# Sliding-window attention into a GEGLU block, groups 2 to 5, second half of the output products: two products change places, the sums' additions and one mask move down the vector engine's queue

## The chip, the cores and the metric

The kernel runs on one core of one Trainium2 chip. The time is the device time of one launch in microseconds (us). A core has five engines with a queue each: PE (matrix multiplications into the 8 banks of PSUM), DVE (vector), ACT (scalar, with the function tables), POOL and SP, which here mostly issue DMAs. Every queue is worked off in the order in which it was written; an instruction whose semaphore is not there yet holds up all behind it on its engine.

## The reference, cut to what matters

```
scores = q @ k.T / sqrt(64)                     # 8 batches, 8 heads, 576 positions, head size 64
scores = scores - slope[h] * (i - j)   where 0 <= i - j < 128, else -1e9
attn   = softmax(scores)                        # rows divided by their sums
x      = (attn @ v), heads side by side         # 4608 tokens x 512
out    = (gelu(x @ w_gate) * (x @ w_val)) @ w_out     # 512 -> 1536 -> 512
```

## The kernel before, in words

The attention works in batches `b` of 576 tokens, the feed-forward block in groups `g` of 512 tokens (nine groups). `xT` holds the attention's result transposed, as a ring of 1536 tokens. Since 576 is not 512, a group's last tokens belong to the next batch: group g+1 needs the first `urgent = 512*(g+2) - 576*(g+1)` tokens of batch g+1, that is 320, 256, 192 and 128 for g = 2, 3, 4, 5. The order of the work on every engine is the order of the Python code (`manual_schedule`); nothing is reordered.

One group has two parts. First come 12 feature tiles (`gate_val`, line 631): four matmuls with `wg` into one bank, four with `wv` into another, then gelu on ACT (L655) and the product `hT` on DVE (L656); tiles 6 to 9 are done together by `gate_quad` with seven products in place of eight (L831 to L878; its sums of `xT` are made on POOL, L789, after tile 3's `hT`). Then comes the product with `w_out`, for groups 2 to 8 also with seven products (`product`, L741 to L752, six matmuls of 128x256 each), for each half `a` of the group's rows. They collect in three banks: products 1, 6, 7, 4 in x, 5 and 3 in y, 2 in z. `gather_out` (L891) takes results out between them, and a bank goes on collecting afterwards:

- p1, u2: copies of x (L898, L900). c11: DVE adds z to what p1 left (L902).
- p5: ACT copies y (L906). c22: DVE adds x, after product 7, to it (L908).
- c21: ACT copies x after product 4 (L910). c12: DVE adds y after product 3 (L913); it is the last reader of y, as c21 is of x.

Into the second half (a = 1, lines 1240 to 1270) are woven: the scores of batch b = g+2 for head pairs 2 and 3 (`scores2`; its list A of ten steps holds the exponentials on ACT, L236, and the masks on DVE, L241: A[2], A[4], A[8], A[9] are masks, the others exponentials); the additions `add(b, 0, None, (0,))` (two instructions on DVE, L391, for the softmax sums of batch b; what they write, `T`, is read by the sums' matmuls, L435, in the next group); and `values(b - 1, urgent=urgent)`, 88 small matmuls (L497) for attn @ v of batch g+1 into six banks, four with one head pair c each and two small ones. Ten scalings on DVE (L556) take these out and divide by the sums: first the urgent part of c = 0, 1, 2, 3 (`scale`), then for the same four banks the rest, which belongs to group g+2, and the two small banks (`more`). So the fifth scaling is the last reader of the bank of c = 0.

The DVE order in this stretch is: u2, c11, two additions, A[2], c22, A[4], ten scalings, c12, A[8], A[9], two more additions, and then `hT` of the next group's tile 0. PE's order is: products 2, 6, 5, 7, the 88 matmuls of `values`, products 3 and 4, and then tile 0 of group g+1. Its first matmul reads `xT` of c = 0, all 512 tokens of the group; the urgent scalings write the last of these.

Banks come from a pool of eight (`bank`, L72). The pool's planner lays the program out with a schedule of its own and gives a new tile the bank that this schedule has had free the longest; a matmul that begins a new tile then waits for the last reader of the tile that had the bank. In the program as laid out, the banks come free after `values`, in each of groups 2 to 5, in the order c = 0, c = 1, x, c = 2, c = 3, the two small ones, y. So tile 0 of group g+1 gets the bank of c = 0 for its `wg` matmuls and the bank of c = 1 for its `wv` matmuls, and tile 1 gets the bank of x and that of c = 2. In the planner's order, counted in PE's matmuls, the fifth scaling begins behind the third matmul of product 4 in group 2, behind the first in group 3, just behind the last matmul of product 3 in group 4 and just ahead of that one in group 5; c21 begins one matmul behind the last of product 4 in all four.

Of the kernel before, what the change touches and what calls it, by code (L numbers as in the profile page):

```python
# [36 lines left out]
def kernel(  # L37
# [346 lines left out]
    def add(b, c0, copy=None, what=(0, 2, 1)):  # L384
        hs = slice(2 * c0, 2 * c0 + 4)
        P = Ps[b % 2].rearrange("p h (n y) -> p h n y", y=64)[:, hs]
        to = T.rearrange("p h (n y) -> p h n y", y=64)[:, hs]
        if 0 in what:
            for x in (0, 1):
                half = slice(64 * x, 64 * x + 64)  # L390
                nc.vector.tensor_tensor(  # L391
                    out=to[half, :, x:x + 7:2], in0=P[half, :, 0:10:3], in1=P[half, :, 1:11:3],
                    op=ALU.add)
        if 2 in what:
            nc.vector.tensor_copy(out=to[0:64, :, 8], in_=P[0:64, :, 12])
            nc.vector.tensor_tensor(
                out=to[64:128, :, 8], in0=P[64:128, :, 11], in1=P[64:128, :, 12], op=ALU.add)
        if 1 in what:
            for x in (0, 1):
                half, n = slice(64 * x, 64 * x + 64), 4 - x  # L400
                (copy or nc.vector.tensor_copy)(
                    out=to[half, :, x + 1:x + 2 * n:2], in_=P[half, :, 2:3 * n:3])
# [270 lines left out]
    def store():  # L673
        for args in stores:
            nc.sync.dma_start(**args)
        stores.clear()
# [64 lines left out]
    def product(g, n, a):  # L741
        (l, r), into = FACTORS[n], INTO[n]
        first = n in (1, 2, 5)
        if first:
            made[g, a, into] = bank()[:, 0:256]
        cols = slice(128 * a, 128 * a + 128)
        x = wo.rearrange("p (i e) (h t) -> p i e h t", e=2, h=2)
        for i in range(NF // 2):
            lhsT = left[:, l, i, cols] if isinstance(l, int) else halves(g)[:, i, l[0], l[1], cols]
            rhs = right[:, r, i, :] if isinstance(r, int) else x[:, i, r[0], r[1], :]  # L750
            nc.tensor.matmul(out=made[g, a, into], lhsT=lhsT, rhs=rhs, start=first and i == 0,  # L751
                             stop=i == NF // 2 - 1, skip_group_check=True)  # L752
# [30 lines left out]
    def combine_x(g, lo=0, hi=256, which=range(4), engine=nc.vector):  # L783
        b11, b12, b21, b22, t1, t2, t3, t4 = (t[:, :, lo:hi] for t in tokens(g) + sums_x(g))
        steps = ((t1, b12, b11, ALU.subtract), (t2, b22, t1, ALU.subtract),
                 (t3, b22, b12, ALU.subtract), (t4, b21, t2, ALU.subtract))
        for n in which:
            to, a, b, op = steps[n]
            engine.tensor_tensor(out=to, in0=a, in1=b, op=op)  # L789
# [101 lines left out]
    def gather_out(g, a, what, copy=nc.scalar.copy):  # L891
        x, y, z = (made.get((g, a, n)) for n in "xyz")
        if what == "p1":
            made[g, a, "lo"] = o_pool.tile([128, DM], FP32, name="osb")
            made[g, a, "hi"] = o_pool.tile([128, DM], FP32, name="osb")
        lo, hi = made[g, a, "lo"], made[g, a, "hi"]
        if what == "p1":
            copy(out=lo[:, 0:256], in_=x)  # L898
        elif what == "u2":
            copy(out=lo[:, 256:512], in_=x)  # L900
        elif what == "c11":
            nc.vector.tensor_tensor(out=lo[:, 0:256], in0=z, in1=lo[:, 0:256], op=ALU.add)  # L902
            if g == NG - 1:
                finished(g, a, lo, slice(0, 256))
        elif what == "p5":
            copy(out=hi[:, 256:512], in_=y)  # L906
        elif what == "c22":
            nc.vector.tensor_tensor(out=hi[:, 256:512], in0=x, in1=hi[:, 256:512], op=ALU.add)  # L908
        elif what == "c21":
            copy(out=hi[:, 0:256], in_=x)  # L910
            finished(g, 2 + a, hi)
        elif what == "c12":
            nc.vector.tensor_tensor(out=lo[:, 256:512], in0=y, in1=lo[:, 256:512], op=ALU.add)  # L913
            finished(g, a, lo, slice(256 if g == NG - 1 else 0, 512), nc.scalar if g == NG - 1 and a else None)
# [229 lines left out]
    def exp_table():  # L1144
        nc.scalar.preload_act_table_set("natural_log_exp_and_others")
# [4 lines left out]
    def out_products(g):  # L1150
        b = g + 2
        O = lambda what, a, copy=act: gather_out(g, a, what, copy)
        P = lambda n, a: product(g, n, a)
        if b > B:
            last = [(4, ("c21",)), (3, ("c12",))]
            for n, after in [(1, ("p1",)), (2, ()), (6, ("u2", "c11")), (5, ("p5",)), (7, ("c22",))] + (
                    last if g == NG - 1 else last[::-1]):
                for a in (0, 1):
                    P(n, a)
                    for what in after:  # L1160
                        O(what, a)
                store()
                if n == 6 and g + 1 < NG:
                    combine_x(g + 1)
            return
        P(1, 0)
        P(2, 0)
        O("p1", 0)
        urgent = 512 * (g + 2) - S * (b - 1)
        if b == B:  # L1170
            P(6, 0)
            O("u2", 0)
            O("c11", 0)
            for n in (3, 2):
                combine_left(g, 0, 6, (n,))
            nc.gpsimd.tensor_copy(out=mark, in_=left[0:1, 2, 5, 0:2])
            sums = combine_weights(0)
            for do in sums[:4]:
                do()
            P(5, 0)  # L1180
            O("p5", 0)
            P(7, 0)
            O("c22", 0)
            scale = values(b - 1, later=True)
            P(4, 0)
            O("c21", 0)
            P(3, 0)
            scale[0]()
            scale[1]()
            O("c12", 0)  # L1190
            P(1, 1)
            O("p1", 1)
            store()
            P(2, 1)
            for do in scale[2:]:
                do()
            combine_x(g + 1, 192, 256, engine=nc.gpsimd)
            for do in sums[4:]:
                do()
            O("c11", 1)  # L1200
            P(6, 1)
            O("u2", 1)
            P(5, 1)
            O("p5", 1)
            P(7, 1)
            O("c22", 1)
            P(3, 1)
            O("c12", 1)
            P(4, 1)
            O("c21", 1)  # L1210
            return
        exp_table()
        O("c11", 0)
        lo = 0 if g == 2 else 2
        combine_left(g, lo, 6, (3,))
        later = []
        scores2(b, 0, later)
        A = later[0]
        P(6, 0)
        O("u2", 0, dve)  # L1220
        combine_left(g, lo, 6, (2,))
        P(5, 0)
        for n in (0, 1, 3):
            A[n]()
        O("p5", 0)
        A[2]()
        P(7, 0)
        O("c22", 0)
        A[4]()
        for n in (5, 6, 7):  # L1230
            A[n]()
        P(1, 1)
        P(4, 0)
        P(3, 0)
        O("p1", 1)
        O("c21", 0)
        O("c12", 0)
        A[8]()
        A[9]()
        scores2(b, 2, later)  # L1240
        A = later[1]
        P(2, 1)
        P(6, 1)
        O("u2", 1, dve)
        O("c11", 1)
        add(b, 0, None, (0,))
        P(5, 1)
        for n in (0, 1, 3, 5, 6, 7):
            A[n]()
        O("p5", 1)  # L1250
        A[2]()
        P(7, 1)
        O("c22", 1)
        A[4]()
        store()
        scale, more = values(b - 1, urgent=urgent)
        for do in scale:
            do()
        P(3, 1)
        P(4, 1)  # L1260
        nc.scalar.preload_act_table_set("gelu_and_others")
        O("c21", 1)
        for do in more:
            do()
        O("c12", 1)
        A[8]()
        A[9]()
        add(b, 0, None, (2,))
        put_off.update({0: lambda: add(b, 0, act, (1,)), 1: lambda: add(b, 2, None, (0, 2)),
                        2: lambda: add(b, 2, act, (1,))})  # L1270
# [3 lines left out]
    for g in range(NG):  # L1274
# [86 lines left out]
        if g in PRODUCTS:  # L1361
            out_products(g)
        else:
            for item in steps(g):
                if isinstance(item, int):
                    out_part(g, item)
                else:
                    RUN[item[0]](*item[1:])
            store()
# [34 lines left out]
```

## Time and profile before

| | us |
|---|---|
| median of 3 runs | 328.53 (328.14 to 328.61) |
| the profiled execution's own time | 328.12 |
| its span from first to last instruction | 326.3 |
| PE busy / DVE busy / ACT busy / POOL busy | 317.3 / 251.7 / 218.2 / 197.1 |
| PE's waits at tile 0 of groups 3 to 6 | 0.77, 0.92, 0.71, 0.51 |

A row of the timeline has the start (us from the span's start), the time from the first start to the last end of a run of equal instructions, the engine, the line of the kernel, the operation, output <- input, shapes (partitions x elements) and the count; in brackets stand the idle time of the engine before it and whose semaphore ended it. The rows of one engine may overlap a little: an instruction is shown until its result is written, and the next one starts before that. A row of the waits has the waiting engine and line, whom it waited for, then the total, the number and the longest.

### The profile page before, as it was taken

To read this page: it belongs to the slowest core of one execution; us is meant where nothing else is said; L and a number is where in the kernel's file an instruction comes from. 1 tells how busy PE (TensorE), PEld (TensorE's weight loads), DVE (VectorE), ACT (ScalarE), POOL (GpSimd) and SP (SyncE) were. 2 spreads that over 40 slices of the span, in tenths; PEclk is the share of its full clock that TensorE was granted. 3 is DMA by queue.
4 is the path that set the end of the run, shared out by engine and by line. 5 is a ranking of instruction groups with operands and counts; after the bars stand their busy time and mean duration, and the time that the engine had idled before them with its cause. 6 is when DMAs were issued, how large, how long until landed. Compare 5 with 4: busy or idle time off the path is not lost. (4 is left out here: it accounts for less than half of the span.)

```text
span 326.3 us, 9416 instructions
## 1 busy us (share of the span) xinstructions
PE 317.3 (97%) x3753; PEld 213.6 (65%) x3753; DVE 251.7 (77%) x499; ACT 218.2 (67%) x417; POOL 197.1 (60%) x228
## 2 busy tenths in 40 slices
PE   8899999999999999999989999999999999999995
PEld 4566746575554768466845785578647787788764
DVE  7889676878779887958797679777896856895692
ACT  7884688567798676756955696578667247627641
POOL 5965589294079896289926994496019495410550
PEclk9999999999999999999999999999999999999999
DMA  8999999999999989966996799769205230003003
GB/s 216 166 195 192 201 174 177 139 192 173 122 152 174 151 150 201 143 133 178 182 186 156 168 128 177 133 167 135 100 35 110 40 131 0 2 0 131 0 4 129
DMA packets 149920, 43.57 MB, mean 134 GB/s; under 512 B 133588, under 2 KB 142964, under 8 KB 149876
## 3 DMA queue, kind: packets, MB, share of 16 engines
q0 software_dynamic: 107456, 18.10, 73.7%
q1 hardware_dynamic: 41424, 23.35, 33.7%
q10 hardware_dynamic: 996, 1.53, 2.0%
q8 instruction: 29, 0.48, 0.6%
q14 instruction: 15, 0.12, 0.2%
HBM read 43.65 MB, written 9.53 MB: 163 GB/s over the span
## 5 line engine op out<-in xcount | busy, mean ns | idle before, releaser
L648 PE MATMUL ps<-xT,wg 128*128 128x512 bf16 (+4 forms) x312 | 71.8, 352 | 2.9 <-DVE xT L556 2.9
L648 PE MATMUL ps<-xT,wv 128*128 128x512 bf16 (+4 forms) x312 | 71.7, 352 | 0.0
L655 ACT ACTIVATE gelu<-ps 128x512 bf16<-128x512 f32 (+3 forms) x77 | 41.6, 546 | 41.7 <-PE ps L648 38.7
L656 DVE TENSOR_TENSOR hT<-ps,gelu 128x512 bf16<-128x512 f32 (+3 forms) x77 | 47.0, 625 | 21.3 <-PE ps L648 15.7
L236 ACT ACTIVATE P<-ps 128x512 bf16<-128x512 f32 (+1 forms) x108 | 51.9, 578 | 4.8 <-PE ps L307 2.5
L648 PEld LDWEIGHTS <-wv 128*128 128x128 bf16 x312 | 29.4, 98 | 29.9 <-DMA wv<-in_moe_w_val_dram 0.3
L648 PEld LDWEIGHTS <-wg 128*128 128x128 bf16 x312 | 28.4, 98 | 30.1 <-DVE xT L556 4.0
L241 DVE TENSOR_TENSOR P<-P,emask 128x768 bf16<-128x768 bf16 x60 | 32.0, 553 | 7.1 <-ACT P L236 5.3
L751 PEld LDWEIGHTS <-hT 128*128 128x128 bf16 x336 | 32.3, 98 | 7.2 <-issue 0.6
L117 POOL DMA_DIRECT2D vb<-in_v_dram x40 | 34.0, 890 | 3.7 <-DMA wo<-in_moe_w_out_dram 1.0
L876 POOL TENSOR_TENSOR hT<-qT,qs 128x512 bf16<-128x512 f32 x10 | 11.5, 1170 | 27.9 <-ACT qs L842 27.9
L117 POOL DMA_DIRECT2D ks<-in_k_dram x30 | 25.4, 885 | 2.8 <-DMA qs<-in_q_dram 2.8
L831 PEld LDWEIGHTS <-kept 128*128 128x128 bf16 x256 | 25.1, 98 | 2.9
L1328 POOL COPY mark<-hT 1x2 bf16<-1x2 bf16 x5 | 0.9, 176 | 42.4 <-DVE hT L656 42.4
L117 POOL DMA_DIRECT2D qs<-in_q_dram x30 | 25.4, 863 | 1.7 <-DMA wo<-in_moe_w_out_dram 1.0
L751 PEld LDWEIGHTS <-left 128*128 128x128 bf16 x252 | 23.8, 98 | 3.7 <-issue 0.4
L751 PE MATMUL ps<-right,hT 128*128 128x256 bf16 x168 | 22.2, 272 | 0.5 <-DVE osb L908 0.2
L839 DVE TENSOR_TENSOR qT<-ps,qT 128x512 f32<-128x512 f32 x20 | 12.9, 686 | 12.5 <-PE ps L831 12.5
L751 PE MATMUL ps<-wo,hT 128*128 128x256 bf16 x168 | 21.0, 273 | 0.0
L751 PE MATMUL ps<-right,left 128*128 128x256 bf16 x168 | 20.6, 273 | 0.2 <-issue 0.2
L839 DVE TENSOR_TENSOR P<-ps,P 128x512 f32<-128x512 f32 x24 | 15.0, 682 | 7.1 <-PE ps L831 7.1
L831 PE MATMUL ps<-xT,wg 128*128 128x256 bf16 x160 | 19.1, 273 | 0.0
(173 smaller groups left out, 616.5 us busy)
## 6 DMA issues: line engine op xcount, KB each, us to landing
out_dram<-osb SPq DMA_DIRECT2D x34, 256.0 KB
rb<-rd SPq DMA_DIRECT2D x8, 576.0 KB
vb<-in_v_dram POOLq DMA_DIRECT2D x32, 128.0 KB, 6.6
qs<-in_q_dram POOLq DMA_DIRECT2D x24, 128.0 KB, 5.5
ks<-in_k_dram POOLq DMA_DIRECT2D x24, 128.0 KB, 7.5
wo<-in_moe_w_out_dram POOLq DMA_DIRECT2D x4, 384.0 KB, 12.1
wg<-in_moe_w_gate_dram POOLq DMA_DIRECT2D x5, 256.0 KB, 9.5
wv<-in_moe_w_val_dram POOLq DMA_DIRECT2D x5, 256.0 KB, 10.1
```

The costliest lines, as they stand in the source:

```text
L117: nc.gpsimd.dma_start(out=t[at:at + n, j, :].rearrange("p (h d) -> p h d", h=H), in_=src[b][:, 128 * j:128 * j + n, :].rearrange("h p d -> ...
L236: nc.scalar.activation(out=dst, in_=src, func=AF.Exp, scale=0.125)
L241: nc.vector.tensor_tensor(out=dst, in0=dst, in1=m, op=ALU.mult)
L648: nc.tensor.matmul(out=ps[:, a:e], lhsT=w[:, c, 128 * f:128 * (f + 1)], rhs=xT[:, c, t0 + lo + a:t0 + lo + e], start=begins and a == 0, st ...
L655: nc.scalar.activation(out=gl[:, 0:n], in_=pg, func=AF.Gelu)
L656: nc.vector.tensor_tensor(out=hid[g][:, f, lo:hi], in0=pv, in1=gl[:, 0:n], op=ALU.mult)
L751: nc.tensor.matmul(out=made[g, a, into], lhsT=lhsT, rhs=rhs, start=first and i == 0, stop=i == NF // 2 - 1, skip_group_check=True)
L831: nc.tensor.matmul(out=ps[:, 256 * e:256 * e + 256], lhsT=w[:, c, at:at + 128], rhs=x[:, c, :], start=n in (1, 2, 5) and e == 0 and c == 0 ...
L839: nc.vector.tensor_tensor(out=to[u], in0=cut(banks[n, u], to[u].shape[1]), in1=to[u], op=ALU.add)
L876: nc.gpsimd.tensor_tensor(out=out, in0=P5[u], in1=high, op=ALU.mult)
L1328: nc.gpsimd.tensor_copy(out=mark, in_=hid[g][0:1, f, 510:512])
```

## The change

Three things are moved in the second half of the output products, in groups 2 to 5. The two additions go from behind c11 to behind c22. The mask A[4] goes from behind c22 to behind the ten scalings, ahead of c12. Product 4 is put ahead of product 3. The instructions themselves stay the same. In the code c21 stays behind both products and ahead of `more` (another engine's queue), and c12 behind A[4].

```diff
         O("u2", 1, dve)
         O("c11", 1)
-        add(b, 0, None, (0,))
         P(5, 1)
         for n in (0, 1, 3, 5, 6, 7):
             A[n]()
         O("p5", 1)
         A[2]()
         P(7, 1)
         O("c22", 1)
-        A[4]()
+        add(b, 0, None, (0,))
         store()
         scale, more = values(b - 1, urgent=urgent)
         for do in scale:
             do()
+        P(4, 1)
         P(3, 1)
-        P(4, 1)
         nc.scalar.preload_act_table_set("gelu_and_others")
         O("c21", 1)
         for do in more:
             do()
+        A[4]()
         O("c12", 1)
         A[8]()
         A[9]()
```

## The prediction

> **What bounds the kernel now.** I read the page's busy shares first, then PE's waits, then the timeline around the end of group 3, then the same places of groups 2, 4 and 5.
>
> ```profile
> PE 317.3 (97%) x3753; PEld 213.6 (65%) x3753; DVE 251.7 (77%) x499; ACT 218.2 (67%) x417; POOL 197.1 (60%) x228
> ```
>
> ```profile
> PE ps L648 <- DVE xT L556: 2.9, 4, 0.9
> ```
>
> PE is the bound: it is busy for 97% of the span. What can be won at all lies in its idle time, and a third of that is one wait that comes four times, 2.9 us together: the first matmul of tile 0 of a group waits for a scaling. The timeline at the end of group 3 shows the place:
>
> ```profile
> 157.64 0.82 PE L751 MATMUL ps<-wo,left 128*128 128x256 bf16 x6
> ...
> 158.50 0.42 DVE L913 TENSOR_TENSOR osb<-ps,osb 128x256 f32<-128x256 f32 x1 [1.09 <-PE ps L751]
> ...
> 161.19 0.82 PE L751 MATMUL ps<-right,hT 128*128 128x256 bf16 x6
> 161.39 1.38 DVE L391 TENSOR_TENSOR T<-P 64x1024 bf16<-64x1024 bf16 x2
> ...
> 162.79 0.56 DVE L241 TENSOR_TENSOR P<-P,emask 128x768 bf16<-128x768 bf16 x1
> 163.27 0.41 DVE L908 TENSOR_TENSOR osb<-ps,osb 128x256 f32<-128x256 f32 x1
> ...
> 163.47 0.83 PE L751 MATMUL ps<-wo,left 128*128 128x256 bf16 x6
> 163.61 0.55 DVE L241 TENSOR_TENSOR P<-P,emask 128x768 bf16<-128x768 bf16 x1
> ...
> 164.07 3.13 DVE L556 TENSOR_TENSOR xT<-ps,rb 128x256 bf16<-128x256 f32 x10
> 164.14 0.82 PE L751 MATMUL ps<-right,hT 128*128 128x256 bf16 x6
> 164.99 0.37 ACT L910 COPY osb<-ps 128x256 f32<-128x256 f32 x1 [1.46 <-PE ps L751]
> ...
> 165.87 1.04 PE L648 MATMUL ps<-xT,wg 128*128 128x512 bf16 x4 [0.92 <-DVE xT L556]
> ...
> 166.74 1.03 PE L648 MATMUL ps<-xT,wv 128*128 128x512 bf16 x4
> ...
> 167.12 0.41 DVE L913 TENSOR_TENSOR osb<-ps,osb 128x256 f32<-128x256 f32 x1
> ```
>
> To be seen: PE ends product 4 at 164.14 + 0.82 = 164.96 and stands until 165.87, while DVE runs from the additions to c12 without a gap (the two additions, A[2], c22, A[4], ten scalings). So in this stretch DVE is what PE waits for. Which of the ten scalings it is, the single rows of the fifth one tell, in groups 2, 3, 4 (with the fourth ahead of it) and 5:
>
> ```profile
> 130.98 0.34 DVE L556 TENSOR_TENSOR xT<-ps,rb 128x192 bf16<-128x192 f32 x1
> ```
> ```profile
> 165.40 0.41 DVE L556 TENSOR_TENSOR xT<-ps,rb 128x256 bf16<-128x256 f32 x1
> ```
> ```profile
> 199.36 0.34 DVE L556 TENSOR_TENSOR xT<-ps,rb 128x192 bf16<-128x192 f32 x1
> ```
> ```profile
> 199.62 0.48 DVE L556 TENSOR_TENSOR xT<-ps,rb 128x320 bf16<-128x320 f32 x1
> ```
> ```profile
> 233.64 0.55 DVE L556 TENSOR_TENSOR xT<-ps,rb 128x384 bf16<-128x384 f32 x1
> ```
>
> and PE's and DVE's rows at the same places of groups 2, 4 and 5:
>
> ```profile
> 126.84 0.82 PE L751 MATMUL ps<-right,hT 128*128 128x256 bf16 x6
> ...
> 129.39 3.13 DVE L556 TENSOR_TENSOR xT<-ps,rb 128x320 bf16<-128x320 f32 x10
> ...
> 129.79 0.82 PE L751 MATMUL ps<-right,hT 128*128 128x256 bf16 x6
> ...
> 131.38 1.04 PE L648 MATMUL ps<-xT,wg 128*128 128x512 bf16 x4 [0.77 <-DVE xT L556]
> ```
> ```profile
> 195.68 0.82 PE L751 MATMUL ps<-right,hT 128*128 128x256 bf16 x6
> ...
> 198.56 3.13 DVE L556 TENSOR_TENSOR xT<-ps,rb 128x192 bf16<-128x192 f32 x10
> 198.62 0.82 PE L751 MATMUL ps<-right,hT 128*128 128x256 bf16 x6
> ...
> 200.16 1.04 PE L648 MATMUL ps<-xT,wg 128*128 128x512 bf16 x4 [0.71 <-DVE xT L556]
> ```
> ```profile
> 229.97 0.81 PE L751 MATMUL ps<-right,hT 128*128 128x256 bf16 x6
> ...
> 232.85 3.13 DVE L556 TENSOR_TENSOR xT<-ps,rb 128x128 bf16<-128x128 f32 x10
> 232.93 0.82 PE L751 MATMUL ps<-right,hT 128*128 128x256 bf16 x6
> ...
> 234.25 1.04 PE L648 MATMUL ps<-xT,wg 128*128 128x512 bf16 x4 [0.51 <-DVE xT L556]
> ```
>
> The fifth scaling ends at 131.32, 165.81, 200.10 and 234.19, and each time PE starts 0.06 us behind it. But tile 0 doesn't need what the fifth scaling writes: its tokens are complete with the fourth (in group 4 at 199.36 + 0.34 = 199.70, and only its fourth matmul reads that one). What it does need is the bank of c = 0, whose last reader the fifth scaling is. So the wait is for a bank, and the inputs stand earlier.
>
> The Trainium skill, Perfetto Trace Analysis, § Identifying Performance Opportunities, says that the same gap coming again and again on the engine that should be saturated can mean too little room for the next tile in PSUM or SBUF. The 0.06 us behind the fifth scaling, four times, agree. By that reading a bank that comes free earlier saves the whole wait, 2.7 in the sum below; by the releaser's name alone (xT, a wait for data) only what the scalings gain, 0.8.
>
> **The additions behind c22.** Two instructions, 1.38 us, 1.40 to the next start (161.39 to 162.79), leave the place behind c11; A[2] and c22 move up. A[2]'s exponentials were the first two of six on ACT and are long done. A[2] then starts at 161.39 and c22 could at 161.39 + 0.48 = 161.87, but c22 reads product 7, and that ends at 161.19 + 0.82 = 162.01; a DVE step behind a product starts 0.04 later (157.64 + 0.82 = 158.46, c12 at 158.50). So c22 starts at 162.05, DVE stands 0.18 with the additions and all scalings queued behind, and they follow at 162.05 + 0.34 (the step from c22 to A[4]) = 162.39, the scalings at 163.79. That takes in that A[4] is gone from there (0.46, 163.61 to 164.07). Net in group 3: scalings 0.28 earlier. In groups 4 and 5 the same working gives 195.68 + 0.82 + 0.04 + 0.34 + 1.40 = 198.28 against 198.56, and 232.56 against 232.85: 0.28 and 0.29 earlier. In group 2 product 7 is late: 126.84 + 0.82 + 0.04 + 1.74 = 129.44 against 129.39, so 0.05 later. What the additions write is read only in the next group; nobody waits.
>
> **A[4] behind the scalings.** Its 0.46 us come ahead of c12 now, so c12, A[8], A[9] and the next group's first hT come later by 0.46, less what the scalings gained: 0.51 in group 2, 0.18 after. The cover, in group 3's beginning:
>
> ```profile
> 134.24 0.69 DVE L656 TENSOR_TENSOR hT<-ps,gelu 128x512 bf16<-128x512 f32 x1
> 135.48 0.69 DVE L656 TENSOR_TENSOR hT<-ps,gelu 128x512 bf16<-128x512 f32 x1 [0.54 <-ACT gelu L655]
> ```
> ```profile
> 140.12 0.68 PE L435 MATMUL ps<-T,ones 128*32 128x144 bf16 x32
> ```
>
> DVE's idle 0.54 ahead of the second hT takes 0.51 up, and the sums' matmuls, the first on PE that need the later additions, stand 5 us further on. Without that cover every later hT of tiles 1 to 3 would come 0.5 late, and with it the sums of xT on POOL, which begin on tile 3's hT. That is thinnest in group 6, where DVE has no such gap; POOL's chain there ends in a wait of PE:
>
> ```profile
> 257.86 0.83 PE L751 MATMUL ps<-right,hT 128*128 128x256 bf16 x6 [0.17 <-DVE hT L726]
> ```
>
> Up to 0.18 of lag may show there; I take 0.1. SP's store of c12's result goes out later by as much as c12; nothing in these groups waits for it. POOL's own queue is passed by no step.
>
> **Product 4 ahead of product 3.** The same twelve matmuls. Product 4 adds to x and so waits for c22, which now ends by 162.46, a full 1.0 ahead of 163.47. c21 can start when the first product of the two is through: 163.47 + 0.83 + 0.04 = 164.34, in place of 164.99, and ends at 164.71; c12 gets its input at 164.96, 2 us before DVE comes to it. By itself this saves nothing. But x comes free 0.65 earlier, and that can change whom tile 0 waits for. In the planner's order before, x comes third, behind c = 0 and c = 1. With the swap c21 stands one matmul behind the end of the first product. At 0.11 a matmul (0.67 for six, 163.47 to 164.14), 0.37 for c21 and the fifth scaling's 0.34, 0.41, 0.48 and 0.55, counted from the start of that product's last matmul: x is free at about 0.48 to 0.59 in all four; c = 0 in group 2 at 0.67 to 0.78, in group 3 at 0.52 to 0.63, in group 4 at 0.48 to 0.59, in group 5 at 0.44 to 0.55. So x goes first in group 2 surely, in 3 probably, and in 4 and 5 it is near a tie by these durations; following the planner's order more closely I take x in 4 too, and in 5 leave it open.
>
> Where x goes first, tile 0's wg matmuls take x, free by 164.71, and its wv matmuls the bank of c = 0. The scalings then come in time: in group 3 they are 0.33 apart ((165.40 - 164.07) / 4), so the urgent four end at 164.20 to 165.21 while the matmuls go at 164.96, 165.18, 165.40 and 165.61 (0.87 for four); the fifth ends at 165.54 against the wv matmuls at 165.83. Group 2 is tightest: fourth 131.11 against 131.27, fifth 131.43 with the 0.06 against 131.49. The idle time is then nothing: 0.77, 0.92, 0.71 and 0.51 saved. Where c = 0 stays first, only the scalings' shift counts: idle 0.82, 0.64, 0.43, 0.22.
>
> **The sum.** All four by x: 2.91. With group 5 open, 2.69 to 2.91, less 0.1 given back in group 6: 2.7. PE has no other wait from group 3 on that these steps touch, so the end moves by that. The profiled execution took 328.12 (span 326.3 and 1.8 around it): 325.4. The median of the runs is 0.41 above it, so 328.53 - 2.7 = 325.8 is what I predict. A difference of 0.2% (0.66 us) is about what a measurement of this kernel can tell from none.
>
> **Rivals.** *The bank of c = 0 stays first everywhere*, or the wait is for data after all, as the releaser's name has it: then 0.77 + 0.92 + 0.71 + 0.51 less 0.82 + 0.64 + 0.43 + 0.22 = 0.8 is won, 327.7. For it: in the order before, x is third. Against: the shift by a whole product. *Half and half*, x in groups 2 and 3 only: 2.91 - 0.43 - 0.22, less some of the 0.1, is 2.2, and 326.3. *The change does nothing*: what PE wins at tile 0 it loses again in the same group, to DVE's and POOL's later sums; 328.5. Against: the 0.54 of slack above. *Slower*: c22 now stands ahead of the additions and waits for product 7 on DVE, with the bank unchanged; each 0.1 of wait beyond the 0.46 that A[4] frees starts all scalings 0.1 later. I find waits of 0.18 and, in group 2, 0.51; c12, placed likewise behind its product, shows 1.09. At that wait in all four groups it is 4 x 0.63 = 2.5 us slower, 331.0; it decides above 0.46 in every group, and only group 2's row goes there.
>
> **How the numbers follow.** Forecast (x first in groups 2 to 4 at least) 0.64; half and half 0.13; c = 0 throughout 0.12, of which 0.05 falls within 0.2%; nothing 0.05; slower 0.06. So faster 0.84, same 0.10, slower 0.06. The range: below, the whole 2.91 and some 0.4 for a run's scatter, 325.2; above, half and half and part of the way to 327.7, 327.0. That holds the first two cases and a little of the third.
>
> **What would show it.** Right: no wait of PE for L556 in groups 3 to 5, c21 some 0.65 earlier against the end of the two products and ahead of the fifth scaling's end, tile 0's wv matmuls right behind its wg ones; A[2] directly behind c11, then c22 after a gap of 0.2 (0.5 in group 2), the additions, the scalings 0.3 earlier in groups 3 to 5. Wrong: PE's start still 0.06 behind the fifth scaling (the bank of c = 0), a gap ahead of c22 beyond 0.46, a new wait of PE in tiles 4 to 9, or one in group 6 beyond 0.3.

## The result and the profile after

The changed kernel took 326.04 us (median of seven runs, 325.47 to 326.98), the kernel before in the same session 327.87 (seven runs, 327.24 to 328.61). The ratio is 0.9948, 95% interval 0.9929 to 0.9968: 1.8 us faster, between 1.0 and 2.3. Forecast were 325.8 us and faster; the drop itself was forecast as 2.7, from 328.53, the median of the first three runs. The two profiled executions stand at 328.12 and 326.04, spans 326.3 and 324.3: 2.0 apart.

The page of the changed kernel, busy time of each engine, and PE's queue of instruction packets (packets, MB, share):

```profile
PE 317.6 (98%) x3753; PEld 213.5 (66%) x3753; DVE 250.5 (77%) x499; ACT 218.2 (67%) x417; POOL 197.2 (61%) x228
...
q8 instruction: 29, 0.48, 0.6%
```

PE's waits in the changed kernel (engine, line, waited for: us in total, times, longest); the first lines:

```profile
PE ps L78 <- DVE zeros L933: 1.0, 1, 1.0
PE ps L751 <- issue: 0.5, 1, 0.5
PE ps L751 <- DVE hT L726: 0.3, 1, 0.3
```

The 2.9 us of waiting for L556 are gone from the list. In their place stand two small ones: 0.5 for "issue" (0.2 before) and 0.3 in group 6 (0.2 before). The timeline at the end of group 3 of the changed kernel, against the one in the prediction:

```profile
160.59 0.81 PE L751 MATMUL ps<-right,hT 128*128 128x256 bf16 x6
160.79 0.55 DVE L241 TENSOR_TENSOR P<-P,emask 128x768 bf16<-128x768 bf16 x1
161.20 0.43 ACT L906 COPY osb<-ps 128x256 f32<-128x256 f32 x1
...
161.67 0.42 DVE L908 TENSOR_TENSOR osb<-ps,osb 128x256 f32<-128x256 f32 x1 [0.33 <-ACT osb L906]
162.01 1.38 DVE L391 TENSOR_TENSOR T<-P 64x1024 bf16<-64x1024 bf16 x2
163.07 0.82 PE L751 MATMUL ps<-right,hT 128*128 128x256 bf16 x6
163.41 3.14 DVE L556 TENSOR_TENSOR xT<-ps,rb 128x256 bf16<-128x256 f32 x10
163.72 0.82 PE L751 MATMUL ps<-wo,left 128*128 128x256 bf16 x6
163.92 0.37 ACT L910 COPY osb<-ps 128x256 f32<-128x256 f32 x1 [0.99 <-PE ps L751]
164.38 1.03 PE L648 MATMUL ps<-xT,wg 128*128 128x512 bf16 x4
165.24 1.03 PE L648 MATMUL ps<-xT,wv 128*128 128x512 bf16 x4
```

To be seen: tile 0's wg matmuls follow product 3 by 0.66, without a gap, and c21 (L910) ends at 164.29, just ahead of them: the bank that they take is x's. But two things are not as forecast. c22 (L908) starts at 161.67, 0.04 behind p5's copy on ACT (161.20 + 0.43), and not behind product 7 (160.59 + 0.81 = 161.40); and the scalings, counted from product 7's start, come at 2.82, where they came at 2.88 before.

**How the losses below are counted.** A row's idle time understates what PE loses, since the modelled end of a product lies 0.16 behind the start of a product that follows without a gap (164.38 - 163.72 = 0.66 against 0.82). So I took, for each matmul of PE, its start less its forerunner's start, less the smallest such distance in any profile of this study, and left out what came to less than 0.1. From 118 us on this gives for each profiled execution (us lost by PE; "late code" is told under the experiments; where it and c22 delay the same matmul, in group 3 of e1 and e3, c22's end parts them):

| kernel | ratio to before, 95% | median | tile 0 (wg, wv), groups 3 to 6 | product 4 behind c22 | other products, and group 6 | late code |
|---|---|---|---|---|---|---|
| before | | 327.9 | 3.57 | 0 | 0 | 0.36 |
| changed | 0.9948 (0.9929 to 0.9968) | 326.04 | 0.30 | 0 | 0.76 | 0.85 |
| e1 order alone | 0.9956 (0.9940 to 0.9973) | 326.05 | 0 | 0.79 | 0 | 2.51 |
| e2 DVE moves alone | 1.0017 (1.0006 to 1.0028) | 328.35 | 3.11 | 0 | 0.11 | 0.73 |
| e3 order, mask | 0.9942 (0.9929 to 0.9955) | 325.88 | 0 | 0.81 | 0 | 0.98 |
| e4 POOL early, groups 3 to 6 | 0.9961 (0.9945 to 0.9977) | 326.72 | 0.48 | 0 | 1.49 | 1.41 |
| e5 c22 early | 0.9919 (0.9897 to 0.9940) | 325.24 | 0 | 0 | 0.29 | 1.28 |
| e6 POOL early, 3 to 5 | 0.9955 (0.9940 to 0.9970) | 326.23 | 0.32 | 0 | 0.39 | 1.37 |
| e7 mask stays | 0.9974 (0.9961 to 0.9987) | 326.64 | 2.10 | 0 | 0.74 | 0 |
| e8 changed, code shifted | 0.9942 (0.9927 to 0.9957) | 325.78 | 0.58 | 0 | 0.75 | 0 |
| e9 e5, code shifted | 0.9914 (0.9892 to 0.9935) | 324.48 | 0.10 | 0 | 0 | 0 |
| e10 before, code shifted | 1.0012 (0.9998 to 1.0026) | 328.26 | 3.91 | 0 | 0 | 0 |

The changed kernel's 0.30 + 0.76 + 0.85 = 1.91 against 3.57 + 0.36 = 3.93 makes 2.02. The two spans differ by 2.0, of which some 0.16 lies ahead of group 2 (its first product starts at 116.67 in place of 116.83), so the account is good to 0.1 or 0.2. Runs of one kernel differ by up to 2 us, so medians that lie 0.3 apart are not told apart below.

### The profile page after: what moved, and what is told of

Same layout as the page of the kernel before. It is cut to its first block, busy times and chain, and to the rows that moved or that the text cites. A ratio compares the mean times of both kernels' runs of the same rounds, so it can differ in the third digit from the quotient of the medians.

```text
span 324.3 us, 9416 instructions
## 1 busy us (share of the span) xinstructions
PE 317.6 (98%) x3753; PEld 213.5 (66%) x3753; DVE 250.5 (77%) x499; ACT 218.2 (67%) x417; POOL 197.2 (61%) x228
## 3 DMA queue, kind: packets, MB, share of 16 engines
q10 hardware_dynamic: 996, 1.53, 2.0%
## 5 line engine op out<-in xcount | busy, mean ns | idle before, releaser
L656 DVE TENSOR_TENSOR hT<-ps,gelu 128x512 bf16<-128x512 f32 (+3 forms) x77 | 46.2, 623 | 17.4 <-PE ps L648 13.7
```

The costliest lines, as they stand in the source:

```text
L656: nc.vector.tensor_tensor(out=hid[g][:, f, lo:hi], in0=pv, in1=gl[:, 0:n], op=ALU.mult)
```

## The experiments

The theory at the start: the bank is the whole gain; the two moves on DVE bring nothing. Its rival: each part carries its share, as the prediction's sum had it.

**e1: the order of the products alone.**

```diff
+        P(4, 1)
         P(3, 1)
-        P(4, 1)
```

> Product 4 ahead of product 3, nothing else; additions and mask stay where they were. Theory (the bank is the whole gain, and the two moves on DVE cost more than they bring, because c22 then waits for p5's copy on ACT with the additions behind it and DVE comes 0.4 to 0.6 later to the next group's work): the waits of PE for L556 (2.9 us) are gone as in the changed kernel; the scalings start 2.55, 2.88, 2.88, 2.88 behind product 7's start as before; DVE comes earlier to the next group, so POOL's chain (which starts behind the gate's fourth hidden tile) too, and product 5's late starts in groups 4 and 5 (0.12, 0.33) and the two of group 6 (0.29, 0.10) mostly go. 0.5 to 1.0 us below the changed kernel: 325.0 to 325.5. Rival (each part carries its share, as the prediction's sum had it): 0.8 or more above the changed kernel, 326.8 to 327.4.

Measured: 0.9956, 326.05 us, the same as the changed kernel. The order alone wins all that the change wins, so the rival falls; but the theory's further 0.5 to 1.0 didn't come. Product 4 adds into the bank that c22 reads, and with the additions ahead of c22 it has to wait. Group 4 of e1, DVE and PE:

```profile
197.36 0.42 DVE L908 TENSOR_TENSOR osb<-ps,osb 128x256 f32<-128x256 f32 x1
```
```profile
196.03 1.60 PE L497 MATMUL ps<-P,vb 64*64 64x192 bf16 x88
197.83 0.81 PE L751 MATMUL ps<-right,hT 128*128 128x256 bf16 x6 [0.20 <-DVE osb L908]
```

c22 ends at 197.78 and product 4 starts at 197.83; unhindered it starts 1.53 behind the first attention matmul, 197.56. In groups 3 to 5 together that costs 0.79. So the additions' move, which does nothing for the scalings, does something that the prediction counted as free: it gets c22 out of product 4's way. The other part of what was missing in e1's profile is this, the timeline of PE in group 2:

```profile
124.42 0.93 PE L751 MATMUL ps<-right,left 128*128 128x256 bf16 x7
127.06 0.71 PE L751 MATMUL ps<-right,left 128*128 128x256 bf16 x5 [1.71 <-issue]
```

PE stops between the seventh and the eighth of the twelve matmuls of products 6 and 5, which nothing on another engine can explain. More on it at e8.

**e2: the DVE moves alone** (additions and mask as in the changed kernel, products 3, 4 in the old order).

> Additions behind c22 and the mask behind the scalings, products in the old order. Theory: PE still waits for the fifth scaling at the end of groups 2 to 5, 0.06 behind its end, with the scalings within 0.15 of where they were (about 2.66, 2.82, 3.01, 2.82 behind product 7's start); behind them DVE is 0.4 to 0.6 later, which costs up to 0.3 a group at POOL's chain: 327.9 to 328.8, so 0 to 0.9 slower than before. Rival (scalings 0.28 earlier in groups 3 to 5, as the prediction's sum had it): 0.8 faster than before, 327.1.

Measured: 1.0017 (1.0006 to 1.0028), 328.35 us. The theory holds, the rival is out. PE's waits in e2:

```profile
PE ps L648 <- DVE xT L556: 2.3, 3, 1.1
```

Counted by starts, the four groups lose 1.22, 0.29, 1.00 and 0.60. Without the bank the moves win nothing.

**e3: the order and the mask,** the additions left behind c11.

> Product 4 ahead of product 3 and the mask behind the scalings; the additions stay behind c11. Theory: c22 has no new wait (the additions cover p5's copy), so the scalings start 0.46 earlier than before: 2.1, 2.4, 2.4, 2.4 behind product 7's start; wv of tile 0 no longer waits for the fifth scaling (0.19 and 0.15 in groups 2 and 4 of the changed kernel), and DVE comes to the next group's first hidden tile about as in the kernel before (7.4 and 7.7 behind product 7's start): 0.6 to 1.1 us below the changed kernel, 324.9 to 325.4, and 0 to 0.3 below the run with the order of the products alone. Rival (the additions' move carries part of the gain): not below the changed kernel, 326.0 or more.

Measured: 0.9942, 325.88 us: not to be told from the changed kernel. In its profile the scalings are in time and tile 0 loses nothing, nor does anything in the gate or in group 6; but product 4 loses 0.81 to c22, as in e1. The expectation had overlooked that as well.

**e4 and e6: POOL's chain let go one hidden tile earlier,** in groups 3 to 6 (e4, below) and in groups 3 to 5 only (e6).

```diff
-            if f == (0 if g == 2 else 3):
+            if f == (0 if g == 2 else 2):
```

The reason is group 5's first half. DVE and PE rows ahead of product 7 (of the first half, reading right and hT), before and then changed:

```profile
221.88 0.56 DVE L726 TENSOR_TENSOR left<-hT 128x768 bf16<-128x768 bf16 x1
...
223.89 0.42 DVE L900 COPY osb<-ps 128x256 f32<-128x256 f32 x1
...
224.37 0.81 PE L751 MATMUL ps<-right,hT 128*128 128x256 bf16 x6
```
```profile
220.12 0.56 DVE L726 TENSOR_TENSOR left<-hT 128x768 bf16<-128x768 bf16 x1 [0.44 <-POOL hT L878]
...
222.13 0.42 DVE L900 COPY osb<-ps 128x256 f32<-128x256 f32 x1
...
222.60 0.81 PE L751 MATMUL ps<-right,hT 128*128 128x256 bf16 x6
```

In the changed kernel DVE waits 0.44 for POOL, u2's copy (L900) comes late behind that, ends at 222.55, and product 7, which adds into the bank that u2 reads, starts at 222.60, 0.25 late. (The expectations call it product 5; by its operands it is product 7.) POOL's chain began with the mark at 207.17 against 208.60: 1.43 earlier, where PE was 2.25 earlier (tile 0 at 197.91 against 200.16).

> The changed kernel with POOL's chain of groups 3 to 6 let go one hidden tile earlier (the mark and combine_x behind tile 2 in place of tile 3, some 1.7 us). Theory (part of the gain is given back by POOL's chain, which follows DVE's queue and not PE): product 5 of groups 4 and 5 starts without the 0.12 and 0.33, group 6 without most of its 0.29 and 0.10; 0.5 to 0.8 below the changed kernel, 325.2 to 325.5. Rival (what is lost in the groups is not POOL's: PE's own gaps, or DVE's queue by itself): within 0.2 of the changed kernel. If POOL's earlier additions slow DVE's while they run together, above it.

> The changed kernel with POOL's chain let go behind tile 2 in groups 3 to 5 only; group 6 as it was. Theory: product 5 of groups 4 and 5 starts without the 0.13 and 0.25, and the 0.8 that PE stood in group 6 in the run with all four groups changed doesn't come: 325.5 to 325.8. Rival (POOL's earlier additions cost DVE as much in groups 3 to 5 as they win): 326.0 to 326.8, with new waits of PE on DVE in groups 3 to 5.

Measured: e4 0.9961, 326.72 us; e6 0.9955, 326.23. In both profiles product 7 of groups 4 and 5 starts without its 0.13 and 0.25, so that reading is right. In the time it doesn't show, and both forecasts were missed: e6's profile lost 1.37 to late code, and medians 0.2 apart tell nothing here. e4 paid for it in group 6. DVE, POOL and PE there:

```profile
241.16 1.34 DVE L789 TENSOR_TENSOR ks<-xT,ks 128x384 bf16<-128x384 bf16 x1
242.43 1.31 DVE L789 TENSOR_TENSOR ks<-xT 128x384 bf16<-128x384 bf16 x1
243.66 1.30 DVE L789 TENSOR_TENSOR ks<-xT,ks 128x384 bf16<-128x384 bf16 x1
```
```profile
241.14 1.15 POOL L789 TENSOR_TENSOR left<-xT 128x512 bf16<-128x512 bf16 x1
242.37 1.16 POOL L789 TENSOR_TENSOR left<-xT,left 128x512 bf16<-128x512 bf16 x1
243.48 1.27 POOL L789 TENSOR_TENSOR left<-xT 128x512 bf16<-128x512 bf16 x1
```
```profile
245.62 0.60 PE L831 MATMUL ps<-xT,wg 128*128 128x256 bf16 x4 [0.60 <-DVE hT L656]
```

The same addition on DVE took 0.35 in the changed kernel, where POOL was still idle:

```profile
241.06 0.35 DVE L789 TENSOR_TENSOR ks<-xT,ks 128x384 bf16<-128x384 bf16 x1
```

Here each ends 0.21 behind one of POOL's (242.50 behind 242.29, 243.74 behind 243.53, 244.96 behind 244.75), and PE waits 0.60 for the hidden tile behind them.

**e7: the changed kernel with the mask back ahead of the scalings.**

```diff
         O("c22", 1)
+        A[4]()
         add(b, 0, None, (0,))
```

(and gone from behind `more`.)

> The changed kernel with the mask A[4] back ahead of the scalings. Theory (the fifth scaling is just in time in the changed kernel, 0.15 late for wv of tile 0 in two groups): all scalings 0.47 later, and wv of tile 0 waits 0.3 to 0.6 in each of four groups: 1.4 to 1.8 above the changed kernel, 327.4 to 327.9. Rival (the bank alone counts, and wv's place has slack): 326.0 to 326.5.

Measured: 0.9974, 326.64 us, 0.26% above the changed kernel, some 0.9 us (0.6 by the medians; the two intervals overlap a little); forecast 1.4 to 1.8. PE loses 2.10 at tile 0 in place of 0.30, but mostly not where the theory had it: wv loses 0.49 of that and wg 1.61. The rows of group 2:

```profile
131.08 3.14 DVE L556 TENSOR_TENSOR xT<-ps,rb 128x320 bf16<-128x320 f32 x10
131.63 1.56 PE L648 MATMUL ps<-xT,wg 128*128 128x512 bf16 x4
```

The four wg matmuls take 1.56 where they take 1.03 without a wait, and each starts some 0.05 behind the end of one of the four urgent scalings. So with the bank of x free the next limit is the data, and close behind. On the other side DVE is through earlier behind the scalings, and product 7 of groups 4 and 5 (0.13, 0.25) and the first of group 6's two (0.28) lose nothing. (The 0.74 in the table is mostly, 0.64, in group 2's first half, ahead of the mask.) So the mask's move is a trade: it wins 1.8 and costs 0.66 later.

**e5: c22 early, with the additions as filler.** What e1 to e3 and the changed kernel leave open can be had together: c22 wants something ahead of it on DVE while p5's copy runs (the additions), but not so much that product 4 waits. So the order and the mask as changed, the additions back behind c11, and A[2] behind c22.

```diff
         O("p5", 1)
-        A[2]()
         P(7, 1)
         O("c22", 1)
+        A[2]()
```

> Product 4 ahead of 3 and the mask behind the scalings as in the changed kernel; the additions stay behind c11, and A[2] goes behind c22 in their place. Theory (c22 has two masters: it waits for p5's copy on ACT, and product 4, which adds into the bank that c22 reads, waits for c22; best is c22 early with something ahead of it that fills the wait): c22 comes 0.48 earlier than with the order and the mask alone, so product 4's wait for it in groups 4 and 5 (0.2 each by the waits) is gone, and the scalings still start about 2.1 to 2.4 behind product 7's start, so wv of tile 0 doesn't wait either. PE then stands only where its code is late (0 to 1.9 and 0 to 0.9 in the profiles so far): 325.0 to 325.7, 0.3 to 0.8 below the changed kernel. Rival (what is left is set by something else than these two waits): as the changed kernel or the run with the order and the mask, 325.9 to 326.1.

Measured: 0.9919 (0.9897 to 0.9940), 325.24 us, as expected, though the interval still overlaps the changed kernel's. The waits at tile 0, for c22, at product 7 and in group 6 are all gone from the profile. What is left of them is 0.29 at a product of group 2's first half, ahead of all that was changed, and 1.28 of late code.

**e8, e11, e12, e10: the late code.** PE's program has 7,506 matmuls and weight loads and comes in 29 packets of 16 KB (the page's q8, above; the page doesn't name its engine, but 0.48 MB is 64 bytes for each of the 7,506, and PE goes on behind its landings). In the nine profiles with the program in its old place (before, changed, e1 to e7) PE stops at the same two places, whatever the kernel: ahead of the eighth of the twelve matmuls of products 6 and 5 in group 2 in five of them (0.36 to 1.88 us), and ahead of the first matmul behind the attention's in group 3 in seven (0.2 to 1.4). In e1 the packet of group 2 lands at 125.84 and PE goes on at 127.06; in the changed kernel 125.17 and 126.43. The two places lie 511 matmuls apart, with their weight loads 1,022 instructions; at 64 bytes each that is four packets, to a few instructions. e8 shifts the program by 32 instructions:

```diff
-    keep_busy(held[0], 7, 512, zeros[:, 0:1].to_broadcast((128, 512)))
-    keep_busy(held[0], 2, 128)
+    keep_busy(held[0], 4, 512, zeros[:, 0:1].to_broadcast((128, 512)))
+    keep_busy(held[0], 21, 64)
```

> The changed kernel with 16 more warm-up matmuls of 64 columns at its start (and three long ones fewer), so that everything behind stands 32 instructions later in PE's program. Theory (PE stops in the middle of a product, at the same matmul in every profile, because a 16 KB packet of its own program lands late): the two places move 16 matmuls ahead, into the scores of the second half of group 2 (some 1.3 us ahead of where it was) and into the attention's matmuls (L497) ahead of product 4 in group 3, and no product is broken at its eighth matmul any more; the time 326 to 327. Rival (a wait for data or for the sums): PE stops at the same matmuls of the same products as in the changed kernel.

Measured: 0.9942, 325.78 us. Both stops are gone, where I expected them to move; the packet of group 2 now lands at 117.09, 8 us ahead of its use, that of group 3 at 161.17, some 1.6 ahead. That speaks against the rival, but doesn't show a stop following the code. e11 and e12 shift it by 8 instructions only (one long warm-up matmul and two short ones replaced by seven of 64 columns; the four short ones left out):

> The changed kernel with four warm-up matmuls more: all code behind stands 8 instructions later. Theory (PE stops where a 16 KB packet of its program ends): the stop that sat ahead of product 4's first matmul in group 3 (0.2 to 1.4 in seven of nine profiles) comes four matmuls earlier, among the attention's matmuls (L497), and the one ahead of the eighth matmul of product 6 in group 2 comes at its fourth, where either shows at all. Rival (a wait for a bank or for data): ahead of product 4's first and product 6's eighth matmul, as before.

> The changed kernel with four warm-up matmuls fewer: all code behind stands 8 instructions earlier. Theory: the stop of group 3 comes inside product 4, at its fifth matmul, and that of group 2 at the twelfth matmul of the row of product 6 and its forerunner, where either shows at all. Rival: at the same matmuls as in the changed kernel.

Measured, one run each: 326.35 us and 325.44. e12 shows no stop in either place, so it says nothing. In e11 the timeline of PE in group 2 reads:

```profile
124.49 0.49 PE L751 MATMUL ps<-right,left 128*128 128x256 bf16 x3
126.26 1.14 PE L751 MATMUL ps<-right,left 128*128 128x256 bf16 x9 [1.27 <-issue]
```

The stop stands behind the third of the twelve matmuls and no longer behind the seventh, four matmuls earlier, with its packet landing at 124.73; and group 3's (0.16) sits four matmuls ahead of product 4, among the attention's. It goes with the code's place and not with the data: shown.

e10 gives the kernel before the same shift as e8.

> The kernel before with the 16 warm-up matmuls more, nothing else. Theory (late code is no part of the change; it is drawn anew in each execution and clouds both kernels): the stop of 0.2 at the eighth matmul of product 6 is gone, PE still waits four times for L556: 327.2 to 327.7, up to 0.5 below the kernel before, and 1.6 to 2.5 above the changed kernel with the shift (325.8): the change without its noise. Rival (the shift itself makes the kernel slower or faster by its warm-up): more than 0.5 off the kernel before.

Measured: 1.0012 (0.9998 to 1.0026), 328.26 us: not faster, against the expectation. The stop is gone, yet PE's wait at tile 0 grew by as much:

```profile
PE ps L648 <- DVE xT L556: 3.2, 4, 1.1
```

Group 2's loss there is 1.28 in place of 0.94 (0.34 more, for the 0.36 that was gone). In e2 the same is seen in group 3, 0.73 of late code and 0.29 of wait. So in the kernel before the late code cost nothing: it lay inside the wait for the fifth scaling. In the changed kernel there is no such wait, and by its profile it counts in full; the medians with and without the shift, 325.78 and 326.04, lie too near to show it. Without it on either side the change is worth 0.9942 / 1.0012 = 0.993, about 2.3 us (1.6 to 3.0 with the two intervals), and PE's losses differ by 3.91 - 0.58 - 0.75 = 2.6.

**e9: e5 with the shift.**

> The run with c22 early (order of the products, mask behind the scalings, A[2] behind c22, additions behind c11) with the 16 warm-up matmuls more. Theory: PE's waits at tile 0 (L556), for c22, and in the gate (L726, product 5) are gone as they were there, and the two late pieces of code too, as in the changed kernel with the shift: 0.7 to 1.1 below the changed kernel with the shift (325.8), so 324.7 to 325.1. Rival (the shift brings nothing by itself, or moves the late code elsewhere): 325.2 or more, with PE waiting for issue inside a product of group 2 to 5.

Measured: 0.9914 (0.9892 to 0.9935), 324.48 us, the lowest median of the study, a little under the forecast. It is faster than the kernel before; its interval overlaps the changed kernel's (0.9929 to 0.9968) by 0.0006, and it is not told from e5. PE's waits in e9:

```profile
PE ps L78 <- DVE zeros L933: 1.0, 1, 1.0
PE ps L497 <- issue: 0.8, 1, 0.8
PE ps L221 <- DVE kT L167: 0.2, 1, 0.2
PE ps L751 <- DVE osb L908: 0.2, 1, 0.2
```

Nothing is left in groups 2 to 6 above 0.2; the 0.8 lies in the kernel's first 118 us.

## Why the prediction was right, and where it failed

**The wait is for a bank: right.** Tile 0 starts at 164.38, while the fifth scaling runs until past 165; in all four groups it follows product 3 without a gap. In the program as laid out the first bank handed out is x's, in all four groups, group 5 too, which was left open. The rival with c = 0's bank throughout is out. A small part of the other two limits is there: the fifth scaling of group 4 and the fourth of group 2, rows of the changed kernel,

```profile
198.39 0.48 DVE L556 TENSOR_TENSOR xT<-ps,rb 128x320 bf16<-128x320 f32 x1
```
```profile
130.84 0.48 DVE L556 TENSOR_TENSOR xT<-ps,rb 128x320 bf16<-128x320 f32 x1
```
```profile
131.37 0.38 PE L648 MATMUL ps<-xT,wg 128*128 128x512 bf16 x1
```

The fifth ends at 198.87, and wv of tile 0 starts at 198.93, 0.15 late: again a bank. In group 2 the fourth ends at 131.32, 0.05 ahead of 131.37, where the fourth wg matmul, which reads it, starts 0.15 late: data. The prediction had called group 2 the tightest.

**The size at tile 0: too small.** 2.91 was the idle time; the loss by starts is 3.57. Won were 3.27.

**The additions behind c22: the step that failed.** The prediction said "c22 reads product 7" and made it wait 0.18 for that. It left out that c22 also adds to what p5 has copied, on ACT behind six exponentials. c22 waited 0.33 in groups 3 and 5, 0.52 in group 4 and 0.80 in group 2, where product 7, held up by late code, ended behind p5's copy (127.79 against 127.55). The prediction's own sign of being wrong, a gap ahead of c22 beyond 0.46, so came in two groups. From product 7's start the scalings come at 2.66, 2.82, 3.01, 2.82, where they came at 2.55, 2.88, 2.88, 2.88: nothing won, in place of 0.28 in three groups. Why c22 stands 0.2 behind p5's end in group 4 in all profiles with the additions moved stays open. That the same move frees c22 for product 4 was counted at nothing ("a full 1.0 ahead"), and is worth 0.8 (e1, e3).

**A[4] behind the scalings: sized from the wrong start.** The lag was measured against product 7 and set off against DVE's idle 0.54. But PE itself comes 0.7 to 0.9 earlier to the next group, counted from product 7's start, and DVE doesn't: the first hT of group 3 comes at 8.00 (134.97 - 126.97) in place of 7.40 (134.24 - 126.84). The rows of the changed kernel:

```profile
126.97 0.82 PE L751 MATMUL ps<-right,hT 128*128 128x256 bf16 x6
```
```profile
134.97 1.29 DVE L656 TENSOR_TENSOR hT<-ps,gelu 128x512 bf16<-128x512 f32 x2
```

POOL's chain, which begins on tile 3's hT, falls behind PE, and product 7 of groups 4 and 5 and two products of group 6 give back 0.76. The prediction had 0.1, and a new wait there as its sign of being wrong; the rival in which all is lost to DVE's and POOL's later sums named the place rightly and the size wrongly.

**Late code: not in the sum at all.** 0.49 more of it counted in the profile of the changed kernel. So 3.27 - 0.76 - 0.49 = 2.02 in the profiles, 1.8 in the medians, and 2.7 forecast. The drop was forecast half as large again as it came out. That the forecast of 325.8 still lay 0.2 from the measured 326.04 was in part luck: it started from a baseline of 328.53 that further runs put at 327.9.

**The rival that ended slower** had its mechanism half right: c22 did stand longer on DVE with the additions and scalings behind it. It needed the bank unchanged; e2 is that case, and it is slower by some 0.5 us, not 2.5.

## What to carry to other kernels

When a wait on the bounding engine disappears, ask what it had been hiding there and which engine does not move ahead with it: here late code and POOL's chain took back over a third of what was won at tile 0, in the profile of the changed kernel (0.49 and 0.76 of 3.27). A step that is moved up to shorten a queue stands on all its inputs, so list every one, with the engine that makes it and what that engine does first; and give a waiting instruction a filler that is just long enough (e5). Read a wait's releaser as the last reader of a buffer too: a change in the order of two products that reads the same data can be worth more than any saving on the engine that is named.

## What the runs showed of the hardware

PE's own program arrives late: at fixed instructions PE stops for 0 to 1.9 us, differently in each profile, and goes on 1.2 to 1.6 us behind the landing of a 16 KB packet of its program. With a shift of 32 instructions both stops went: the packets then landed 8 us and some 1.6 us ahead of their use (e8). Why the packets come late where they do was not tried. The Trainium skill, Runtime: NRT & Kernel Launch, § Instruction fetch mechanics, has code coming in 16 KiB blocks whose fetch is mostly hidden; the 29 packets of 0.48 MB agree with the blocks, and the 1.71 us of e1 don't agree with hidden.

DVE's additions of bf16 in SBUF went from 0.35 to 1.3 us while POOL ran its own additions (e4). The Trainium skill, SBUF — State Buffer, § SBUF: two separate sides, tells of a port pair that DVE and GpSimd share by an exclusive lock, held for a whole instruction; e4's rows, where each DVE addition ends 0.21 behind one of POOL's, agree.
